# FFN tiles of 512 tokens from batch 1 on; local products one position at a time on GpSimd, sums of rows on VectorE

## The chip, the cores and the metric

The kernel runs on one core of one Trainium2 chip. The metric is the device time of one execution in microseconds; the time of a kernel is the median of its runs.

## What is computed

Eight batches of 576 tokens, eight heads of 64. Attention is the sum of a global part on rows pooled by four and a local part on the seven nearest keys; a low-rank mix over the tokens and an FFN with residual follow. All is float32.

```python
# attention, per batch and head: q, k, v are [576, 64]
q_d, k_d, v_d = (t.reshape(144, 4, 64).mean(axis=1) for t in (q, k, v))
out_up = repeat(softmax(q_d @ k_d.T / 8) @ v_d, 4)        # pooled by 4, repeated
mask = abs(pos[:, None] - pos[None, :]) < 4
out_local = softmax(where(mask, q @ k.T / 8, -1e9)) @ v
x = concat_heads(out_up + out_local)                       # [8, 576, 512]
# mix and FFN: U [576, 32], V [32, 576], w_ch1 [512, 2048], w_ch2 [2048, 512]
u = x + ((x.T @ U) @ V).T
out = u + maximum(u @ w_ch1, 0) @ w_ch2
```

## The kernel before

**FFN.** The 4608 tokens are cut into tiles, of 288 tokens in batches 0 and 1 (`NB = 2`), of 384 from batch 2 on: 4 and 9 tiles. A tile runs 16 steps, one for each 128 columns of the hidden layer. A step has `ffn1`, twelve matmuls into one bank `ps_h` (L956: four pieces `dc` of u, each as w-high x u-high, w-high x u-low, w-low x u-high), then on ScalarE the relu `hH` (L964), on VectorE the remainder `hL` (L965), and `ffn2`, twelve matmuls into the four banks `acc` (L981, three for each). `ffn2` of step i stands about `LAG` = 3 steps behind its `ffn1`. From step `H1 = NFC + LAG` on, `ps_h` alternates between two banks. `hH` has four buffers, `hL` three. At the end of a tile GpSimd adds u-high and u-low (L991), VectorE adds `acc` (L994), and the chunk `o` goes to the output. u lies in `uH` and `uL`, two buffers each.

**Attention.** Work comes in pairs of heads, four pairs a batch. The four pairs of batch 0 take an early path; the other 28 go through `late_global`, `local_attn` and `mix_part`, each pair so:
- q and k arrive as `gq` and `gT`; GpSimd adds rows by four in two steps (`pool_halves`: `gh`, then `smq` or `smk`, L440 and L442); v arrives as `vr` for each head and is added in two steps (L530, L532) into `vs`.
- TensorE makes the pooled and the local scores (L790, L783), VectorE the maximum `mx` (L540), ScalarE the exponentials `E`; TensorE transposes E (L555), multiplies by `vs` (L569); VectorE scales the result into `od` (L573); SyncE stores it to `up_s` in six DMAs (L579). The local scores go through `se` to memory and come back by position as `sc`.
- `local_attn`: nine positions per partition, `vl` holds 15 rows of v. A softmax over seven scores gives `ms`. For two positions at a time GpSimd multiplies seven rows of `vl` by `ms` into `Pt` (L852, 896 elements, the ninth position alone with 448), ScalarE copies the pooled output `ul` into the eighth place of `Pt` (L846), VectorE sums the eight places into `acc` (L857).
- `mix_part`: the sum goes to memory and comes back in two layouts; `xT` (transpose, L921), `ps_hu` (L931), then `ps_u` (the u matmul, L739), VectorE adds (L743), ScalarE writes u-high (L746), GpSimd u-low (L748).

**Order.** The program records operations with an engine, an estimated duration, a priority and the keys they read and write. A planner (`Plan.run`) simulates five engines with these numbers and issues the operations in the order it finds. Attention has lower priority numbers than the FFN matmuls, so an attention matmul goes first as soon as the plan takes it for ready, and FFN blocks fill the rest. A buffer of a pool is handed out in recorded order when its last user is done. SyncE issues every DMA. On the chip each engine works through its queue in the planned order.

**Deadlines.** The first `ffn1` of a tile reads u of all four pairs of every batch in it. Piece `dc` of u is written by pair `dc`, and the twelve matmuls take the pieces in order.

## Time and profile before

| | |
|---|---|
| time, median of 3 runs (lowest to highest) | 1010.79 us (1009.43 to 1011.28) |
| the profiled execution: its time, its span | 1003.93 us, 1002.2 us |
| TensorE: busy, share | 976.2 us, 97% |
| GpSimd | 571.7 us, 57% |
| VectorE | 438.3 us, 44% |
| ScalarE | 347.1 us, 35% |
| first matmul of the FFN, first of tile 2 | 63.15 us, 198.83 us |

Span is from the first to the last instruction of the profiled execution. Busy time of TensorE counts matmuls that overlap in its pipeline, so what a matmul costs is read from the distance of blocks in the chain, not from its own duration. "Idle before" and "waited" name what came last of the things that an instruction waited for. L956 is line 956 of the kernel before; in the changed kernel the same work has other line numbers (L949 ffn1, L974 ffn2, L958 hL, L742 the u matmul, L848 the products, L853 their reduce).

### The profile page before, as it was taken

Reading aid. Unit: us, or ns where it says so; the run is one execution under the profiler, and the core shown is the slowest. Engines: PE = TensorE matmul, PEld = TensorE weight load, DVE = VectorE, ACT = ScalarE, POOL = GpSimd, SP = SyncE. Lnnn points to the kernel's source line nnn. Section 1 sums busy time; section 2 is a strip of 40 time slices with the busy share of each in tenths; the row PEclk is TensorE's granted clock in tenths of the full one; section 3 lists DMA queues with packets and bytes.
Section 4 is the critical chain, followed back from the end, with each engine's and each line's share of the span. In section 5 each row is a group of like instructions: output and inputs, shape, how many; then the busy total and the mean of one; then the engine's idle time right before and its main releaser. Section 6 shows DMA issues by size and latency. Waiting matters only on the chain.

```text
span 1002.2 us, 24561 instructions
## 1 busy us (share of the span) xinstructions
PE 976.2 (97%) x9896; PEld 942.6 (94%) x9896; DVE 438.3 (44%) x814; ACT 347.1 (35%) x1012; POOL 571.7 (57%) x640
## 2 busy tenths in 40 slices
...
GB/s 265 317 186 210 205 154 155 154 162 137 131 121 111 130 167 130 132 105 179 144 116 128 102 137 144 83 127 113 113 150 72 32 56 24 32 2 1 32 1 32
DMA packets 220906, 120.04 MB, mean 120 GB/s; under 512 B 174052, under 2 KB 196920, under 8 KB 220792
## 3 DMA queue, kind: packets, MB, share of 16 engines
...
q14 instruction: 36, 0.29, 0.1%
...
## 4 chain that ended last, share of the span: by engine, by line
PE 86%; DMA 2%; POOL 1%; DVE 1%; ACT 1%; SPq 1%; issue 0%; DVEq 0%; ACTq 0%
PE ps_h L956 38%; PE acc L981 38%; PE ps_a L569 2%; PE ps_b L790 2%; DMA wr<-in_W 2%; PE ps_b L783 2%; PE ps_t L555 2%; PE ps_hu L931 2%; POOL Pt L852 1%; PE ps_u L739 1%; DMA vr<-in_v 1%; SPq L806 1%; DVE acc L857 0%; ACT half L347 0%; ACT E L544 0%
## 5 line engine op out<-in xcount | busy, mean ns | idle before, releaser
L981 PE MATMUL acc<-hH,W 128*128 128x384 f32 (+1 forms) x1664 | 442.3, 327 | 0.0
L956 PE MATMUL ps_h<-uH,W 128*128 128x384 f32 (+1 forms) x1376 | 360.4, 323 | 3.9 <-DVE hL L965 2.9
L981 PEld LDWEIGHTS acc<-hH,W 128*128 128x128 f32 x1664 | 297.3, 188 | 2.4
L981 PE MATMUL acc<-hL,W 128*128 128x384 f32 (+1 forms) x832 | 268.0, 322 | 0.0
L852 POOL TENSOR_TENSOR Pt<-vl,ms 128x896 f32<-128x896 f32 (+1 forms) x140 | 239.6, 1790 | 28.4 <-DMA vl<-in_vp 14.0
L956 PEld LDWEIGHTS ps_h<-uH,W 128*128 128x128 f32 x1376 | 246.3, 190 | 5.7 <-DVE hL L965 3.5
L965 DVE SCALAR_TENSOR_TENSOR hL<-ps_h,hH 128x384 fp32r<-128x384 f32 (+1 forms) x208 | 108.9, 524 | 324.1 <-ACT hH L964 323.8
L964 ACT ACTIVATE hH<-ps_h 128x384 fp32r<-128x384 f32 (+1 forms) x208 | 97.3, 468 | 366.8 <-PE ps_h L956 358.9
L956 PE MATMUL ps_h<-uL,W 128*128 128x384 f32 (+1 forms) x688 | 221.7, 322 | 1.1 <-POOL uL L748 1.1
L857 DVE TENSOR_REDUCE acc<-Pt 128x128 f32<-128x1024 f32 (+1 forms) x140 | 152.8, 1108 | 62.3 <-ACT Pt L846 27.1
L981 PEld LDWEIGHTS acc<-hL,W 128*128 128x128 f32 x832 | 156.7, 188 | 0.0
L956 PEld LDWEIGHTS ps_h<-uL,W 128*128 128x128 f32 x688 | 130.6, 190 | 1.7 <-POOL uL L748 1.7
L956 PE MATMUL ps_h<-u,W 128*128 128x384 f32 x432 | 98.1, 334 | 0.0
L923 POOL TENSOR_TENSOR xL<-xL,xH 116x640 fp32r<-116x640 f32 x28 | 43.9, 1567 | 73.4 <-ACT xH L922 66.8
L846 ACT ACTIVATE Pt<-ul 128x128 f32<-128x128 f32 (+1 forms) x140 | 56.6, 433 | 81.7 <-DVE acc L857 54.9
L991 POOL TENSOR_TENSOR o<-uH,uL 128x384 f32<-128x384 f32 (+1 forms) x43 | 39.0, 940 | 70.0 <-DMA out_t<-o 70.0
L956 PEld LDWEIGHTS ps_h<-u,W 128*128 128x128 f32 x432 | 76.9, 188 | 0.0
L748 POOL TENSOR_TENSOR uL<-xT,uH 128x384 fp32r<-128x384 f32 (+2 forms) x52 | 41.0, 808 | 56.7 <-ACT uH L746 56.7
L530 POOL TENSOR_TENSOR vr<-vr 72x256 f32<-72x256 f32 x56 | 41.2, 736 | 52.4 <-DMA vr<-in_v 51.7
L362 POOL TENSOR_TENSOR W<-c,W 128x512 fp32r<-128x512 f32 x32 | 41.0, 1289 | 14.3 <-ACT W L358 14.3
L743 DVE TENSOR_TENSOR xT<-ps_u,xT 128x384 f32<-128x384 f32 (+2 forms) x64 | 27.4, 452 | 37.2 <-PE ps_u L739 37.1
L790 PE MATMUL ps_b<-smk,smq 64*32 64x144 f32 x672 | 38.9, 296 | 0.0
...
## 6 DMA issues: line engine op xcount, KB each, us to landing
...
```

The lines of the kernel that those rows point to most:

```text
L362: pool_tt(1.0 * n, lambda: nc.gpsimd.tensor_tensor(out=lo_out(), in0=ta()[l0:], in1=hi_out()[l0:].bitcast(F32), op=ALU.subtract), [t, *own ...
L530: pool_tt(256, lambda x=x: nc.gpsimd.tensor_tensor(out=x()[:, :, 0:2, :], in0=x()[:, :, 0:2, :], in1=x()[:, :, 2:4, :], op=ALU.add), [x], ...
L748: pool_tt(n, lambda uH=uH, uL=uL, uf=uf, us=us: nc.gpsimd.tensor_tensor(out=uL.ap(hp, us), in0=uf(), in1=uH.ap(hp, us).bitcast(F32), op=AL ...
L790: nc.tensor.matmul(pg()[m:m + QL, a * SD:(a + 1) * SD], sq()[o, n:n + QL], sk()[o], start=True, stop=True)
L846: act(n * D, lambda n=n, ps=ps, Pt=Pt: nc.scalar.activation(Pt()[:, :n, :, 7], ul()[:, ps, :], AF.Copy), [ul], [(Pt, 1)], prio, 0.16)
L852: nc.gpsimd.tensor_tensor(out=Pt()[:, :n, :, 0:7].rearrange("p s d o -> p o s d"), in0=win, in1=at()[:, ps, :].rearrange("p s o -> p o s") ...
L857: dve(8.5 * n * D, lambda n=n, ps=ps, Pt=Pt: nc.vector.tensor_reduce(out=acc()[:, ps, :], in_=Pt()[:, :n], axis=AX.X, op=ALU.add), [(Pt, 0 ...
L923: pool_tt(640, lambda: nc.gpsimd.tensor_tensor(out=xL(), in0=xL().bitcast(F32), in1=xH().bitcast(F32), op=ALU.subtract), [xL, xH], [xL], prio)
L956: nc.tensor.matmul(ps()[:, :tn], W1[fc]()[:, w, dc, :], u.ap(dc), start=(n == 0), stop=(n == 3 * NDC - 1))
L964: last_h[i] = act(tn, lambda: nc.scalar.activation(hH()[:, :tn], ps()[:, :tn], AF.Relu), [ps], [hH], FIRST, 0.05)
L965: dve(tn, lambda: nc.vector.scalar_tensor_tensor(hL()[:, :tn], ps()[:, :tn], 0.0, hH()[:, :tn].bitcast(F32), op0=ALU.max, op1=ALU.subtract ...
L981: nc.tensor.matmul(ac[e]()[:, :tn], W2[fc]()[:, w, es], hx()[:, :tn], start=(fc == 0 and n == 0), stop=(fc == NFC - 1 and n == 2))
```

## The change

- **Tiles.** `NB = 1`, `TW = 512`: two tiles of 288 for batch 0, then seven of 512 and a last one of 448, ten in all. u of a tile lies in one buffer (288) or in two halves (512); the buffers of even tiles from 2 on are in pool `loc`, the others in `ffn`, two each. `LAG` is 2, `hH` and `hL` have two buffers.
- **Local part.** One position a time: GpSimd multiplies seven rows of `vl` by `ms` into `Pt` (448 elements, nine times), VectorE sums the seven places into row p of `vl` itself, and when all nine are there, one addition over 576 elements puts `ul` to them. ScalarE's copies are gone. `Pt` shares three buffers (`cT`) with the weight conversion and the output chunks; `vl` and `ul` have two buffers.
- **Sums of four rows** of late pairs: one VectorE reduce each for q, k and v of each head, in place of GpSimd's two additions.
- `od` lies in the first part of `E`; `se` is one buffer instead of two; the plan takes longer durations for three attention blocks of TensorE.

```diff
@@ attn_mix_ffn_kernel
-    TN, TW = 288, 384
-    NT = S // TN
-    NB = 2
+    TN, TW = 288, 512
+    NT = 2
+    NB = 1
...
-    LAG = 3
+    LAG = 2
...
+    def pool_late(raw, lo, out, prio):
+        dve(S, lambda: nc.vector.tensor_reduce(
+            out=out()[:, 0:SD], in_=raw()[:, lo:lo + S].rearrange("p (j r) -> p j r", r=4), axis=AX.X, op=ALU.add),
+            [raw], [out], prio)
...
-        pool_halves(qr, 0, sq, False, prio)
-        pool_halves(kr, (SPAD - S) // 2, sk, False, prio)
+        pool_late(qr, 0, sq, prio)
+        pool_late(kr, (SPAD - S) // 2, sk, prio)
...
-            pool_tt(256, lambda x=x: nc.gpsimd.tensor_tensor(
-                out=x()[:, :, 0:2, :], in0=x()[:, :, 0:2, :], in1=x()[:, :, 2:4, :], op=ALU.add), [x], [x], prio)
-            pool_tt(128, lambda x=x, vs=vs: nc.gpsimd.tensor_tensor(
-                out=vs(), in0=x()[:, :, 0, :], in1=x()[:, :, 1, :], op=ALU.add), [x], [vs], prio)
+            dve(512, lambda x=x, vs=vs: nc.vector.tensor_reduce(
+                out=vs(), in_=x().rearrange("p a r d -> p a d r"), axis=AX.X, op=ALU.add), [x], [vs], prio)
...
-        op(PE, 0.52, t_mm, [(E, a) for a in range(NQ)] + ["ident"], pt, prio)
+        op(PE, 0.6, t_mm, [(E, a) for a in range(NQ)] + ["ident"], pt, prio)
...
-        od = g([128, NQ, D], "od")
+        od = lambda: E()[:, 0:NQ * D].rearrange("p (a d) -> p a d", a=NQ)
...
-        for i in range(2):
+        for i in range(1):
             se = buf(loc, [128, NH * KL + 3], F32, f"se{i}")
...
-        for p0 in range(0, NPOS, 2):
-            n = min(2, NPOS - p0)
-            Pt = buf(loc, [128, 2, D, 8], F32, "Pt", "Pt", 2)
...
+        for p in range(NPOS):
+            Pt = buf(ffn, [128, D, 8], F32, "Pt", "cT:p", 3)
...
+                nc.gpsimd.tensor_tensor(
+                    out=Pt()[:, :, 0:7].rearrange("p d o -> p o d"), in0=vl()[:, p:p + 7, :],
+                    in1=at()[:, p, :].unsqueeze(2).broadcast_to([128, 7, D]), op=ALU.mult)
...
+            dve(7 * D, lambda p=p, Pt=Pt: nc.vector.tensor_reduce(
+                out=vl()[:, p, :], in_=Pt()[:, :, 0:7], axis=AX.X, op=ALU.add), [Pt], [(vl, p)], prio)
+        dve(1.4 * NPOS * D, lambda: nc.vector.tensor_tensor(out=ul(), in0=vl()[:, 0:NPOS, :], in1=ul(), op=ALU.add),
+            [ul] + [(vl, p) for p in range(NPOS)], [ul], prio)
...
-        hH = buf(ffn, [128, TW], F32R, "hH", bufs=4)
-        hL = buf(ffn, [128, TW], F32R, "hL", bufs=3)
+        hH = buf(ffn, [128, TW], F32R, "hH", bufs=2)
+        hL = buf(ffn, [128, TW], F32R, "hL", bufs=LAG)
```

How it moves instructions, at the start of tile 2 first. TensorE's queue before (`ps_hu` and `ps_u` are batch 1's last pair; `W_15` is the last step of tile 1, `W_0` the first of tile 2):

```order
L981 MATMUL acc_2490<-hH,W_15_2124 128x288
L931 MATMUL ps_hu<-xH,Ust 64x128 x5
L931 MATMUL ps_hu<-xL,Ust 64x128 x5
L739 MATMUL ps_u<-Vst,stk 128x288 x2
L956 MATMUL ps_h<-uH,W_0_273 128x288
L956 MATMUL ps_h<-uL,W_0_273 128x288
L956 MATMUL ps_h<-uH,W_0_273 128x288 x2
```

TensorE's queue now, from the same pair's first u matmul on:

```order
L742 MATMUL ps_u<-Vst,stk 128x512
L974 MATMUL acc_2579<-hH,W_14_2244 128x288
L974 MATMUL acc_2579<-hL,W_14_2244 128x288
L974 MATMUL acc_2579<-hH,W_14_2244 128x288
L974 MATMUL acc_2555<-hH,W_15_2305 128x288
L974 MATMUL acc_2555<-hL,W_15_2305 128x288
L974 MATMUL acc_2555<-hH,W_15_2305 128x288
L974 MATMUL acc_2562<-hH,W_15_2305 128x288
L974 MATMUL acc_2562<-hL,W_15_2305 128x288
L974 MATMUL acc_2562<-hH,W_15_2305 128x288
L742 MATMUL ps_u<-Vst,stk 128x64
```

Six more matmuls of `ffn2` follow and then tile 2's first twelve: fifteen matmuls of tile 1 now stand between the pair's first u matmul and the block that reads it.

VectorE's queue in the midst of the attention, from one `hL` to the next, before (384 columns):

```order
L965 SCALAR_TENSOR_TENSOR hL<-ps_h,hH 128x384
L857 TENSOR_REDUCE acc<-Pt 128x128
L936 TENSOR_TENSOR stk<-ps_hu,stk 32x128
L857 TENSOR_REDUCE acc<-Pt 128x128
L857 TENSOR_REDUCE acc<-Pt 128x64
L965 SCALAR_TENSOR_TENSOR hL<-ps_h,hH 128x384
```

and now, one of the fullest such stretches:

```order
L958 SCALAR_TENSOR_TENSOR hL<-ps_h,hH 128x512
L576 TENSOR_TENSOR E<-ps_a,ri 112x192
L834 TENSOR_REDUCE lsm<-ms 128x9
L535 TENSOR_REDUCE vs<-vr 72x128
L836 RECIPROCAL lrl<-lse 128x9
L853 TENSOR_REDUCE vl<-Pt 128x64
L543 TENSOR_REDUCE mx<-ps_b 128x3
L853 TENSOR_REDUCE vl<-Pt 128x64 x4
L535 TENSOR_REDUCE vs<-vr 72x128
L853 TENSOR_REDUCE vl<-Pt 128x64
L958 SCALAR_TENSOR_TENSOR hL<-ps_h,hH 128x512
```

Between two `hL` stand more and smaller operations of a pair, the sums of v among them.

GpSimd's queue, one pair's sums and products before:

```order
L440 TENSOR_TENSOR gh<-gq 128x288
L442 TENSOR_TENSOR smq<-gh 128x144
L440 TENSOR_TENSOR gh<-gT 128x288
L442 TENSOR_TENSOR smk<-gh 128x144
L530 TENSOR_TENSOR vr<-vr 72x2x128
L852 TENSOR_TENSOR Pt<-vl,ms 128x7x128 x2
L852 TENSOR_TENSOR Pt<-vl,ms 128x7x64
```

and now a pair's softmax and its nine products, with no sum near them:

```order
L829 TENSOR_TENSOR ms<-sc,lmx 128x63
L838 TENSOR_TENSOR ms<-ms,lrl 128x63
L848 TENSOR_TENSOR Pt<-vl,ms 128x7x64 x9
L829 TENSOR_TENSOR ms<-sc,lmx 128x63
L838 TENSOR_TENSOR ms<-ms,lrl 128x63
```

The sums have left GpSimd's queue, and the products come in nine pieces instead of five.

## Rows read from the trace of the kernel before

**Rows 1.** The engines' busy time, share of the span and instructions (the page's first part), and the view of cores: span and mean granted TensorE clock.

```profile
PE 976.2 (97%) x9896; PEld 942.6 (94%) x9896; DVE 438.3 (44%) x814; ACT 347.1 (35%) x1012; POOL 571.7 (57%) x640
core 0: 1002.2 us, clock 0.986
```

**Rows 2.** The chain of work that ended last (the page's fourth part): share of the span by engine, then by line.

```profile
PE 86%; DMA 2%; POOL 1%; DVE 1%; ACT 1%; SPq 1%; issue 0%; DVEq 0%; ACTq 0%
PE ps_h L956 38%; PE acc L981 38%; PE ps_a L569 2%; PE ps_b L790 2%; DMA wr<-in_W 2%; PE ps_b L783 2%; PE ps_t L555 2%; PE ps_hu L931 2%; POOL Pt L852 1%; PE ps_u L739 1%; DMA vr<-in_v 1%; SPq L806 1%; DVE acc L857 0%; ACT half L347 0%; ACT E L544 0%
```

**Rows 3.** The same chain in order of time, two neighbouring pieces in tile 9, whose tiles have 384 columns: start us, us, engine, line and matmuls in the piece.

```profile
770.08 2.08 PE ps_h L956 x12
772.16 2.08 PE acc L981 x12
```

**Rows 4.** The chain of the stretch from 200 to 300 us in order of time, two neighbouring pieces in tile 3, with 288 columns; columns as in rows 3.

```profile
287.06 1.60 PE ps_h L956 x12
288.65 1.58 PE acc L981 x12
```

**Rows 5.** The timeline of TensorE at the start of tile 2: start us, us, engine, line, operation, out<-in; in brackets the idle time before and what ended it.

```profile
198.50 0.50 PE L739 MATMUL ps_u<-Vst,stk 128*128 128x288 f32 x2 [1.55 <-DVE stk L936]
198.83 0.29 PE L956 MATMUL ps_h<-uH,W 128*128 128x288 f32 x1
...
201.22 0.40 PE L956 MATMUL ps_h<-uH,W 128*128 128x288 f32 x1 [1.03 <-ACT uH L746]
202.21 0.41 PE L956 MATMUL ps_h<-uL,W 128*128 128x288 f32 x1 [0.59 <-POOL uL L748]
```

**Rows 6.** Who TensorE waited for from 63 us to the end: engine and line that waited, what ended the wait; us in total, times, longest us. The first, the fourth and the last of eight rows, whose totals sum to 9.4 us.

```profile
PE ps_h L956 <- DVE hL L965: 2.9, 2, 2.3
...
PE ps_h L956 <- ACT uH L746: 1.0, 1, 1.0
...
PE ps_t L555 <- DVE xT L743: 0.3, 1, 0.3
```

**Rows 7.** Groups of GpSimd's instructions by line and shape: out<-in, shapes, count, busy us, mean ns of one, and idle time before them with what ended it.

```profile
L852 POOL TENSOR_TENSOR Pt<-vl,ms 128x896 f32<-128x896 f32 x112 | 212.3, 1963 | 27.3 <-DMA vl<-in_vp 14.0 <-DVE acc L857 12.7
...
L530 POOL TENSOR_TENSOR vr<-vr 72x256 f32<-72x256 f32 x56 | 41.2, 736 | 52.4 <-DMA vr<-in_v 51.7 <-PE ps_h L956 0.7
...
L852 POOL TENSOR_TENSOR Pt<-vl,ms 128x448 f32<-128x448 f32 x28 | 30.7, 1095 | 1.1 <-DVE acc L857 1.1
...
L532 POOL TENSOR_TENSOR vs<-vr 72x128 f32<-72x128 f32 x56 | 25.8, 460 | 1.6
L440 POOL TENSOR_TENSOR gh<-gq 128x288 f32<-128x288 f32 x28 | 18.9, 675 | 12.2 <-DMA gq<-in_qT 12.2
L440 POOL TENSOR_TENSOR gh<-gT 128x288 f32<-128x288 f32 x28 | 18.7, 669 | 7.0 <-DMA gT<-in_kT 5.6
...
L442 POOL TENSOR_TENSOR smk<-gh 128x144 f32<-128x144 f32 x32 | 13.7, 427 | 1.5
...
L442 POOL TENSOR_TENSOR smq<-gh 128x144 f32<-128x144 f32 x28 | 11.9, 426 | 1.6
```

**Rows 8.** Groups of VectorE's instructions by line and shape; columns as in rows 7.

```profile
L857 DVE TENSOR_REDUCE acc<-Pt 128x128 f32<-128x1024 f32 x112 | 134.8, 1216 | 60.7 <-ACT Pt L846 27.1 <-POOL Pt L852 25.1 <-issue 4.4
L965 DVE SCALAR_TENSOR_TENSOR hL<-ps_h,hH 128x384 fp32r<-128x384 f32 x144 | 79.9, 555 | 278.2 <-ACT hH L964 278.1
L965 DVE SCALAR_TENSOR_TENSOR hL<-ps_h,hH 128x288 fp32r<-128x288 f32 x64 | 29.0, 453 | 45.9 <-ACT hH L964 45.7
...
L857 DVE TENSOR_REDUCE acc<-Pt 128x64 f32<-128x512 f32 x28 | 18.9, 674 | 1.6 <-POOL Pt L852 1.5
...
L540 DVE TENSOR_REDUCE mx<-ps_b 128x3 f32<-128x432 f32 x28 | 16.9, 604 | 24.3 <-PE ps_b L783 23.9 <-PE ps_b L790 0.4
...
L573 DVE TENSOR_TENSOR od<-ps_a,ri 112x192 f32<-112x192 f32 x28 | 9.8, 351 | 12.2 <-PE ps_a L569 12.1
```

**Rows 9.** Groups of ScalarE's instructions by line and shape; columns as in rows 7.

```profile
L964 ACT ACTIVATE hH<-ps_h 128x384 fp32r<-128x384 f32 x144 | 70.9, 493 | 308.0 <-PE ps_h L956 300.4 <-PE ps_u L739 7.4
L846 ACT ACTIVATE Pt<-ul 128x128 f32<-128x128 f32 x112 | 47.2, 458 | 59.7 <-DVE acc L857 33.0 <-DMA ul<-up_s 25.6 <-POOL xL L923 0.8
...
L846 ACT ACTIVATE Pt<-ul 128x64 f32<-128x64 f32 x28 | 9.3, 333 | 22.0 <-DVE acc L857 21.9
```

**Rows 10.** VectorE's instructions of line 366, each with two SBUF inputs: count, duration ns min/median/max, first and last start us, shapes.

```profile
L366 DVE SCALAR_TENSOR_TENSOR Vst<-cv,Vst x2: 487/638/790, 22.0 to 24.9; 32x288 fp32r<-32x288 f32 x2
L366 DVE SCALAR_TENSOR_TENSOR Ust<-cu,Ust x1: 1200/1200/1200, 67.2 to 67.2; 116x160 fp32r<-116x160 f32 x1
```

**Rows 11.** Two stretches, the first from the FFN's first matmul to tile 2, the second on to the last tile that attention fills: length, then busy us and instructions of PE, PEld, DVE, ACT, POOL, then the granted clock, the DMA engines' share and GB/s.

```profile
63.00:198.80 135.80, 129.76 (x1574) 125.20 (x1574) 81.70 (x152) 67.10 (x190) 112.51 (x127) 0.96 0.74 183
198.80:865.00 666.20, 663.89 (x6517) 647.45 (x6516) 290.99 (x526) 222.00 (x670) 408.62 (x448) 1.00 0.49 115
```

**Rows 12.** Who waited for whom, all engines; columns as in rows 6.

```profile
DVE acc L857 <- POOL Pt L852: 26.6, 36, 2.6
```

**Rows 13.** The timeline of one late pair's od: VectorE's row, then SyncE's issue of the stores (columns as in rows 5).

```profile
445.67 0.35 DVE L573 TENSOR_TENSOR od<-ps_a,ri 112x192 f32<-112x192 f32 x1
446.04 3.81 SPq L579 DMA_DIRECT2D up_s<-od  x6
```

More of the change, by code (lines that the diff above doesn't have):

```diff
@@ L436, in attn_mix_ffn_kernel, with pool_halves @@
     heads = [slice(hh * D, (hh + 1) * D) for hh in range(2)]
-    def pool_halves(raw, lo, out, e, prio):
-        gh = work(e, glo, [128, SD, 2], F32, "gh")
+    def pool_late(raw, lo, out, prio):
+        dve(S, lambda: nc.vector.tensor_reduce(
+            out=out()[:, 0:SD], in_=raw()[:, lo:lo + S].rearrange("p (j r) -> p j r", r=4), axis=AX.X, op=ALU.add),
+            [raw], [out], prio)
+    def pool_halves(raw, lo, out, prio):
+        gh = work(True, early_pool, [128, SD, 2], F32, "gh")
         x4 = lambda: raw()[:, lo:lo + S].rearrange("p (j r) -> p j r", r=4)
@@ L447, in early_global @@
         sk = work(True, glo, [128, SD], F32, "smk")
[L448 to L449 removed]
+        pool_halves(qt, 0, sq, prio)
+        pool_halves(kt, (SPAD - S) // 2, sk, prio)
         od = buf(early_pool, [128, NQ, D], F32, "od_e", None, NOD)
@@ L570, in a_mm @@
                                          start=(c == 0), stop=(c == 1))
-        op(PE, 0.85, a_mm, [(E, "T", 0), (E, "T", 1)] + vss, [pa], prio)
-        od = g([128, NQ, D], "od")
+        op(PE, 1.1, a_mm, [(E, "T", 0), (E, "T", 1)] + vss, [pa], prio)
+        od = lambda: E()[:, 0:NQ * D].rearrange("p (a d) -> p a d", a=NQ)
         dve(NQ * D, lambda: nc.vector.tensor_tensor(
             out=od()[:NP], in0=out()[:NP], in1=ri()[:NP].unsqueeze(2).broadcast_to([NP, NQ, D]), op=ALU.mult),
-            [pa, ri], [od], prio)
+            [pa, ri], [(E, "od")] + [(E, "T", c) for c in range(2)] + [(E, a) for a in range(NQ)], prio)
         def store(hh):
@@ L582, in late_global @@
         for hh in range(2):
-            dma(lambda hh=hh: store(hh), [od], [(up_s, hh)], prio, 160, 1.3)
+            dma(lambda hh=hh: store(hh), [(E, "od")], [(up_s, hh)], prio, 160, 1.3)
         return s_s
@@ L859, in local_attn, with prod @@
-        dma(lambda: nc.sync.dma_start(out=x_s().rearrange("h (c s) d -> (h c) s d", s=NPOS), in_=acc()),
-            [(acc, p) for p in range(0, NPOS, 2)], [(x_s, 0), (x_s, 1)], prio)
+        for p in range(NPOS):
+            Pt = buf(ffn, [128, D, 8], F32, "Pt", "cT:p", 3)
+            def prod(p=p, Pt=Pt):
+                nc.gpsimd.tensor_tensor(
+                    out=Pt()[:, :, 0:7].rearrange("p d o -> p o d"), in0=vl()[:, p:p + 7, :],
+                    in1=at()[:, p, :].unsqueeze(2).broadcast_to([128, 7, D]), op=ALU.mult)
+            rd = [vl, at] + [(vl, i) for i in range(p, min(p + 7, NPOS))]
+            pool_tt(7 * D, prod, rd, [Pt], prio, 1.75)
+            dve(7 * D, lambda p=p, Pt=Pt: nc.vector.tensor_reduce(
+                out=vl()[:, p, :], in_=Pt()[:, :, 0:7], axis=AX.X, op=ALU.add), [Pt], [(vl, p)], prio)
@@ L862, in attn_mix_ffn_kernel @@
+        dve(1.4 * NPOS * D, lambda: nc.vector.tensor_tensor(out=ul(), in0=vl()[:, 0:NPOS, :], in1=ul(), op=ALU.add),
+            [ul] + [(vl, p) for p in range(NPOS)], [ul], prio)
+        dma(lambda: nc.sync.dma_start(out=x_s().rearrange("h (c s) d -> (h c) s d", s=NPOS), in_=ul()),
+            [ul], [(x_s, 0), (x_s, 1)], prio)
     tiles, segs = [], {}
     for g0 in (*range(0, NB * S, TN), *range(NB * S, B * S, TW)):
-        n = TN if g0 < NB * S else TW
+        n = TN if g0 < NB * S else min(TW, B * S - g0)
```

46 lines of the change are left out of this document (13 added, 33 removed).

## The prediction, made before the changed kernel was run

> **What bounds the kernel now.** I read the engines' shares first: TensorE is busy for 97% of the span at a mean granted clock of 0.986, GpSimd 57%, VectorE 44%, ScalarE 35% [rows 1]. Then the chain that ended last: 86% of it is TensorE, and the two FFN matmul lines, L956 and L981, are 38% each [rows 2]. So nearly the whole span is one queue of matmuls that waits for almost nothing: from 63 us on, when the FFN begins, its waits are eight rows that sum to 9.4 us, the largest 2.9 us, the last 0.3 us [rows 6]. The other engines count only where TensorE waits for them. The one place where it does so in a lump is the start of tile 2 at 198.5 us, where batch 1's last pair comes late: 1.55 us before its u matmul, then 1.03 and 0.59 us inside the first ffn1 [rows 5].
>
> What a matmul costs I read off the chain's blocks of twelve. At 384 columns a block takes 2.08 us [rows 3], so 173.3 ns a matmul; 384 columns at the upper clock, 2.4 GHz, are 160.0 ns, which leaves 13.3 ns. At 288 columns a block takes 1.59 us (mean of the two rows) [rows 4], so 132.5 ns, of which 120.0 are columns and 12.5 are left. The remainder hardly depends on the width: it is a price per matmul.
>
> **Fewer, wider matmuls.** Each tile has 16 steps of one ffn1 and one ffn2 block, 32 blocks of twelve. Before: four tiles of 288 and nine of 384, so 4 x 32 x 1.59 + 9 x 32 x 2.08 = 203.5 + 599.0 = 802.6 us. After: two of 288, seven of 512 and a last one of 448. With 13.3 ns a matmul a block of 512 takes 12 x (213.3 + 13.3) = 2.72 us and one of 448 2.40 us: 101.8 + 7 x 32 x 2.72 + 32 x 2.40 = 787.8 us. The term is **-14.7 us**; the columns are the same, 1152 of 4992 matmuls go. No row shows 512 columns. If the remainder grew with the width (2.08 x 512/384 = 2.77 us and 2.43 us), the stage would take 800.6 us and the gain would be 1.9 us; if it stayed at 12.5 ns, 2.71 and 2.39 us, 785.3 us and 17.3 us. I take 13.3 ns: the rows at the two widths differ by 0.8 ns only, and 384 is the nearer.
>
> The Trainium skill (TensorE: Matmul & The Clock Gate, section Back-to-back issue gap) gives N/2.4 + 2.5 ns for an isolated warm matmul. By that the 1152 matmuls would be worth 2.9 us instead of 14.7. The rows above differ from it, 13.3 and 12.5 ns, and the measurement decides; the page's form, columns plus a constant, is the one that they show.
>
> **GpSimd.** Per late pair the products are four of 896 elements at 1963 ns and one of 448 at 1095 ns, 8.95 us; afterwards nine of 448, 9.86 us. What goes are the four-row sums: two vr at 736, two vs at 460, gh at 675 and 669, smq at 426, smk at 427 ns, 4.59 us [rows 7]. Net -3.7 us a pair, about -103 us over 28 pairs: its busy time falls from 572 to about 470 us. In the stretch ahead of tile 2 it was busy for 112.5 of 135.8 us [rows 11], and the last pair of batch 1 ran through it, so this is where its relief counts: the order now has the last pair's u matmul ahead of fifteen matmuls of ffn2, not right ahead of tile 2's first block. They are 15 x 132.5 ns = 2.0 us, and the first nine of the twelve ffn1 matmuls don't read that pair, 9 x 226.6 ns = 2.0 us more of cover. The wait of tile 2's start goes: **-3.2 us** (0 if VectorE only takes GpSimd's place there).
>
> **VectorE.** It gets what the others lose. Before, a pair's reduces are four of 1216 and one of 674 ns, 5.54 us. From the two forms, (1216 - 674)/512 = 1.06 ns an element, a reduce of 448 is an estimated 606 ns and one of 576 742 ns. After: 9 x 0.61 for the products, 2 x 0.74 for q and k, 2 x 0.67 for v, and one addition of 576, from the hL rows (555 + 192 x 1.06) 0.76 us: 9.05 us [rows 8]. That is +3.5 us a pair, about +98 us; busy some 535 us. From 198.8 to 865 us it was busy for 291 of 666 us [rows 11]; 22 pairs more make it 57%. By shares there is room. But the order is dense in places: in the piece quoted in the section on the change, between two hL, stand six product reduces, two v sums, a maximum (604 ns) and od (351 ns), 5.9 us, with hL at 512 columns (an estimated 0.69 us) 6.6 us, and two small ones; the step itself is 5.44 us plus attention's matmuls.
>
> The added addition reads two SBUF tensors while GpSimd works. Of the three operations of that kind, one of 160 elements took 1200 ns though two of 288 took 487 and 790 ns [rows 10]. So it may cost up to about 1 us more a pair, on VectorE alone. The Trainium skill (SBUF — State Buffer, section Who interferes with whom) has a rule that speaks against this piece: a VectorE instruction with two SBUF inputs and a GpSimd instruction that reads SBUF lock each other out; the 1200 ns fit it. No term of the sum hangs on it.
>
> **What pays for that.** hH has two buffers instead of four: the relu of step i may start only when ffn2 of step i-2 has ended, and its bank is wanted two blocks later, after 5.44 us. ReLU (493 ns at 384 columns, so at most 0.66 us) and hL (0.69 us) leave about 4.1 us [rows 8, 9]; before it was three blocks of 2.08 less 1.05, 5.2 us. A delay of VectorE above 4.1 us stops TensorE. I charge **+2 us**: a third of the 6.2 us of waits that are left once tile 2's are gone; bounds 0 and, if these waits triple, +12.
>
> **Edits that I cost at nothing.** ScalarE's copies into Pt, 458 and 333 ns, 56.5 us in all [rows 9], go; TensorE waited for ScalarE once, 1.0 us [rows 6]. od now lies in E: it was written at 445.67 us and its six stores were issued until 449.85 us [rows 13], so the next pair's exponentials may wait some 4 us plus the landing; cover is the FFN block that TensorE always has, without it each pair would lose that. The products share three buffers with the output chunks: at eight tile ends they wait for a store. One band buffer instead of two, 16-step tiles with LAG 2 and 40 output stores for 52 change nothing on TensorE; the 64 u matmuls stay 64. The deadline of attention stays loose: batch 2's last u matmul for tile 3 stands after step 10 of tile 2, five steps or 27 us early.
>
> **Sum.** -14.7 - 3.2 + 2.0 = -15.9 us. The profiled execution took 1003.93 us, its span 1002.2 and 1.7 around it, so 988 us for one like it; the median of the runs, 1010.79, lies 6.9 us above that execution, and I carry the difference over unchanged: **995 us**.
>
> **Rivals.** *The width pays per column.* Then 1.9 + 3.2 us are won: 1005.7 us. For it: no row at 512. Against it: 12.5 and 13.3 ns. The skill's 2.5 ns would end near the same place, 1004.7 us.
> *New waits eat the gain in part or whole.* TensorE stands 8 to 11 us more than I charge, 1003 to 1006 us, or some 14 to 18, 1009 to 1013 us. For it: dense stretches of VectorE as above. Against it: before, GpSimd was as full (112.5 of 135.8 us), and TensorE hardly waited.
> *VectorE paces the FFN.* Place: hL behind the product reduces in VectorE's queue. A product takes 1095 ns and its reduce 606 ns, so a reduce that stands too early in the queue waits 0.49 us for each product, 4.4 us a pair, and hL stands behind it; before, reduces already waited 26.6 us for products, up to 2.6 us at a time [rows 12]. It decides from 4.1 us a step on; if each of the 24 pairs of batches 2 to 7 costs TensorE 1.3 us (half of that longest wait), it is 31 us, and the time 1010.8 - 17.9 + 31 = 1024 us, slower. Below 0.75 us a pair it stays faster. Against it: between the reduces stand other operations, and 57% is no bound.
>
> **How the numbers follow.** My forecast 0.70; per column 0.06; the gain eaten in part 0.05, eaten whole 0.05; slower by VectorE 0.11; 0.03 for an end below 985 us. What a measurement can tell from no change is about 0.2%, 2 us, so faster means below 1008.8 us: 0.70 + 0.06 + 0.05 + 0.03 = 0.84; same 0.05; slower 0.11. The range: the low end takes 17.3 and 3.2 us, no charge, and 5 us won of what else the first 200 us lose, 985 us; the high end takes in the per-column case and the part-eaten one, 1006 us. What lies outside is 0.11 + 0.05 + 0.03 = 0.19.
>
> **What would show it.** Right: in the chain, blocks of twelve at 2.72 us; no wait over 0.5 us at tile 2's first block; GpSimd near 470, VectorE near 535 us; TensorE's waits from 63 us on below 12 us; a span near 986 us. Wrong: blocks above 2.75 us (per column), or rows in which ps_h or a matmul of attention waits for hL, vs, smq or smk for more than 20 us together (VectorE).

## The result, and the profile after

The changed kernel took 1017.15 us (median of 4 runs, 1015.15 to 1018.32) where the kernel before took 1010.20 (4 runs, 1009.43 to 1011.28). The ratio is 1.0077, 95% interval 1.0052 to 1.0102: slower by 0.8%, where 995 us had been forecast. The profiled execution took 1018.32 us.

The engines' shares, the chain's share by engine and the clock of the changed kernel, to be read beside [rows 1, 2]:

```profile
PE 977.1 (96%) x8744; PEld 817.1 (80%) x8744; DVE 535.0 (53%) x1006; ACT 289.6 (28%) x824; POOL 459.4 (45%) x514
PE 62%; DMA 8%; DVE 6%; SPq 5%; POOL 5%; issue 3%; ACT 1%; DVEq 0%; ACTq 0%; POOLq 0%
core 0: 1016.5 us, clock 0.981
```

VectorE's 535 and GpSimd's 459 us are near the 535 and 470 us of the prediction. The chain is another: TensorE's share of it fell from 86% to 62%, and DMA, VectorE, SyncE's queue and GpSimd came in. The two stretches of [rows 11], of after (the boundary is again tile 2's start):

```profile
66.80:212.40 145.60, 136.37 (x1700) 130.25 (x1699) 113.35 (x222) 61.45 (x179) 97.86 (x107) 0.94 0.80 192
212.40:843.90 631.50, 621.71 (x5229) 503.31 (x5228) 351.28 (x648) 167.07 (x493) 306.31 (x339) 1.00 0.50 115
```

Tiles 0 and 1, which the change doesn't resize, take 145.6 us in place of 135.8, with VectorE at 113.4 of them (81.7 before) and the clock at 0.94 (0.96). By the ends of these windows, 3.8 us are lost up to the first FFN matmul, 9.8 in tiles 0 and 1, and 0.7 from there to the end: 14.3 us in all. That is more than the 7 us between the medians, since the first trace of before was 6.3 us under its median and that of after 1.2 us above. Nor are the 9.8 us all lost: the stretch now holds 126 more matmuls (1700 in place of 1574), the attention of one more pair, which later tiles don't have to make room for.

Who TensorE waits for from the FFN's start on (columns as in [rows 6]), the first seven of 13 rows, which sum to 19.5 us in place of 9.4:

```profile
PE ps_t L558 <- DVE xT L746: 3.8, 3, 1.9
PE ps_b L793 <- DVE smk L438: 2.5, 2, 1.6
PE acc L974 <- DVE hL L958: 2.0, 1, 2.0
PE ps_a L572 <- ACT E L561: 2.0, 1, 2.0
PE ps_a L572 <- DVE vs L535: 1.9, 2, 1.5
PE ps_hu L924 <- POOL xL L916: 1.6, 2, 1.1
PE ps_h L949 <- DVE hL L958: 1.4, 3, 0.5
```

14.9 us of them are waits for VectorE (5.8 before). What VectorE itself waits for, its rows with a DMA as releaser, all of the same view:

```profile
DVE vs L535 <- DMA vr<-in_v: 29.4, 18, 5.0
...
DVE lmx L828 <- DMA sc<-s_s: 15.9, 11, 3.2
DVE smq L438 <- DMA gq<-in_qT: 13.6, 9, 3.3
DVE xT L914 <- DMA Y<-x_s: 12.1, 7, 3.9
...
DVE smk L438 <- DMA gT<-in_kT: 5.0, 7, 1.1
...
DVE ul L855 <- DMA ul<-up_s: 3.4, 5, 1.0
```

79.4 us, 57 times, where the same rows of before make 15.3 us, 12 times. One place shows what that does. VectorE's timeline, then TensorE's, then three windows around it (columns as in [rows 5, 11]):

```profile
177.66 1.04 DVE L535 TENSOR_REDUCE vs<-vr 72x128 f32<-72x512 f32 x1 [3.59 <-DMA vr<-in_v]
178.62 0.20 DVE L836 RECIPROCAL lrl<-lse 128x9 f32<-128x9 f32 x1
178.74 0.39 DVE L958 SCALAR_TENSOR_TENSOR hL<-ps_h,hH 128x288 fp32r<-128x288 f32 x1
179.91 0.75 DVE L438 TENSOR_REDUCE smq<-gq 128x144 f32<-128x576 f32 x1 [0.78 <-DMA gq<-in_qT]
180.58 0.81 DVE L746 TENSOR_TENSOR xT<-ps_u,xT 128x512 f32<-128x512 f32 x2
```

```profile
179.19 0.40 PE L974 MATMUL acc<-hL,W 128*128 128x288 f32 x1 [2.04 <-DVE hL L958]
...
181.32 1.49 PE L558 MATMUL ps_t<-ident_sb,E 128*72 128x128 f32 x6 [1.60 <-DVE xT L746]
```

```profile
160.00:179.00 19.00, 17.14 (x235) 16.37 (x233) 13.18 (x30) 5.22 (x20) 10.64 (x13) 1.00 0.73 142
179.00:183.00 4.00, 2.21 (x10) 1.83 (x11) 3.22 (x7) 1.44 (x5) 3.92 (x5) 0.61 1.15 283
183.00:200.00 17.00, 17.00 (x215) 16.50 (x217) 12.39 (x27) 4.24 (x12) 12.53 (x16) 0.89 0.58 136
```

VectorE stands 3.59 us before a sum of v, because its rows haven't landed. hL is the second instruction behind it, so TensorE stands 2.04 us; then the same with q's sum and xT, 1.60 us. The granted clock falls to 0.61 in this window, a mix of its two levels of 1.2 and 2.4 GHz, and is 0.89 in the next 17 us: here the two waits cost more than their length.

VectorE's groups by shape (columns as in [rows 7]), the new ones but smk, which is as smq:

```profile
L853 DVE TENSOR_REDUCE vl<-Pt 128x64 f32<-128x448 f32 x252 | 150.0, 612 | 44.3 <-POOL Pt L848 42.8
...
L535 DVE TENSOR_REDUCE vs<-vr 72x128 f32<-72x512 f32 x56 | 60.9, 1088 | 29.5 <-DMA vr<-in_v 29.4
L855 DVE TENSOR_TENSOR ul<-vl,ul 128x576 f32<-128x576 f32 x28 | 24.4, 870 | 3.9 <-DMA ul<-up_s 3.4
...
L438 DVE TENSOR_REDUCE smq<-gq 128x144 f32<-128x576 f32 x28 | 20.7, 741 | 13.6 <-DMA gq<-in_qT 13.6
```

And the chain in order of time: two neighbouring pieces of tile 7, whose operand lies in u, two of tile 8, in uo, and one of the last tile, with 448 columns (columns as in [rows 3]):

```profile
752.95 2.72 PE ps_h L949 x12
755.67 2.72 PE acc L974 x12
...
910.33 2.79 PE ps_h L949 x12
913.12 2.73 PE acc L974 x12
...
932.44 2.43 PE ps_h L949 x12
```

### The profile page after: what moved, and what is told of

Its sections match the earlier page's. It is cut to its first block, busy times and chain, and to the rows that moved or that the text cites. A ratio compares the mean times of both kernels' runs of the same rounds, so it can differ in the third digit from the quotient of the medians.

```text
span 1016.5 us, 21910 instructions
## 1 busy us (share of the span) xinstructions
PE 977.1 (96%) x8744; PEld 817.1 (80%) x8744; DVE 535.0 (53%) x1006; ACT 289.6 (28%) x824; POOL 459.4 (45%) x514
## 4 chain that ended last, share of the span: by engine, by line
PE 62%; DMA 8%; DVE 6%; SPq 5%; POOL 5%; issue 3%; ACT 1%; DVEq 0%; ACTq 0%; POOLq 0%
PE ps_h L949 28%; PE acc L974 28%; SPq L582 3%; POOL Pt L848 3%; DMA gT<-in_kT 2%; DMA s_s<-se 2%; DVE vl L853 2%; PE ps_a L572 1%; PE ps_t L558 1%; PE ps_hu L924 1%; PE ps_b L793 1%; DVE o L987 1%; DMA vr<-in_v 1%; DMA out_t<-o 1%; PE ps_b L786 1%
## 5 line engine op out<-in xcount | busy, mean ns | idle before, releaser
L974 PE MATMUL acc<-hH,W 128*128 128x512 f32 (+2 forms) x1280 | 409.1, 377 | 0.0
L848 POOL TENSOR_TENSOR Pt<-vl,ms 128x448 f32<-128x448 f32 x252 | 244.6, 1088 | 23.6 <-DMA out_t<-o 10.7
L949 PE MATMUL ps_h<-u,W 128*128 128x512 f32 (+2 forms) x1152 | 242.1, 360 | 1.9 <-DVE hL L958 1.4
L958 DVE SCALAR_TENSOR_TENSOR hL<-ps_h,hH 128x512 fp32r<-128x512 f32 (+2 forms) x160 | 101.2, 633 | 262.8 <-ACT hH L957 260.5
L974 PE MATMUL acc<-hL,W 128*128 128x512 f32 (+2 forms) x640 | 236.8, 370 | 2.0 <-DVE hL L958 2.0
L949 PEld LDWEIGHTS ps_h<-u,W 128*128 128x128 f32 x1152 | 200.7, 192 | 29.3 <-DVE hL L958 2.1
L957 ACT ACTIVATE hH<-ps_h 128x512 fp32r<-128x512 f32 (+2 forms) x160 | 88.4, 552 | 410.6 <-PE ps_h L949 409.8
L949 PE MATMUL ps_h<-uo,W 128*128 128x512 f32 x768 | 189.8, 395 | 0.0
L853 DVE TENSOR_REDUCE vl<-Pt 128x64 f32<-128x448 f32 x252 | 150.0, 612 | 44.3 <-POOL Pt L848 42.8
L949 PEld LDWEIGHTS ps_h<-uo,W 128*128 128x128 f32 x768 | 143.4, 188 | 33.2
L535 DVE TENSOR_REDUCE vs<-vr 72x128 f32<-72x512 f32 x56 | 60.9, 1088 | 29.5 <-DMA vr<-in_v 29.4
L984 POOL TENSOR_TENSOR o<-u 128x512 f32<-128x512 f32 (+2 forms) x24 | 26.5, 1125 | 86.9 <-DMA out_t<-o 82.9
L547 ACT ACTIVATE E<-ps_b,nb 128x144 f32<-128x144 f32 x84 | 31.0, 377 | 25.5 <-DMA up_s<-E 24.1
```

The lines of the kernel that those rows point to most:

```text
L535: dve(512, lambda x=x, vs=vs: nc.vector.tensor_reduce(out=vs(), in_=x().rearrange("p a r d -> p a d r"), axis=AX.X, op=ALU.add), [x], [vs] ...
L547: act(SD, lambda a=a: nc.scalar.activation(Ea()[:, a], pooled_view(ps)[:, a], AF.Exp, bias=nb()[:, a:a + 1], scale=1.0 / 128.0, accum_out= ...
L848: nc.gpsimd.tensor_tensor(out=Pt()[:, :, 0:7].rearrange("p d o -> p o d"), in0=vl()[:, p:p + 7, :], in1=at()[:, p, :].unsqueeze(2).broadca ...
L853: dve(7 * D, lambda p=p, Pt=Pt: nc.vector.tensor_reduce(out=vl()[:, p, :], in_=Pt()[:, :, 0:7], axis=AX.X, op=ALU.add), [Pt], [(vl, p)], prio)
L949: nc.tensor.matmul(ps()[:, :tn], W1[fc]()[:, w, dc, :], u.ap(dc), start=(n == 0), stop=(n == 3 * NDC - 1))
L957: last_h[i] = act(tn, lambda: nc.scalar.activation(hH()[:, :tn], ps()[:, :tn], AF.Relu), [ps], [hH], FIRST, 0.05)
```

## The experiments

Theory 1: the sums moved to VectorE, and their waits, hold up hL and attention, and TensorE waits. Theory 2: the width's gain was lost (uo, early tiles). Other rivals: buffers coupled by the edits; the planner's order. All times are against runs of the kernel before on the same chip (medians 1009.1 to 1010.8), as a ratio with its 95% interval.

**The edits on the old tiles.** In e1 the kernel before gets all attention edits of the diff and keeps its tiles; e2, e3 and e4 get one part each; e12 is e3 with two buffers for Pt alone.

```diff
 e2: -pool_halves(qr, 0, sq, False, prio)   +pool_late(qr, 0, sq, prio)      (and kr; v as in the diff)
 e3: products and their sums as in the diff, Pt in "cT:p"
 e4: -od = g([128, NQ, D], "od")            +od = lambda: E()[:, 0:NQ * D]...  (and one se)
 e12: as e3, -Pt = buf(ffn, ..., "cT:p", 3) +Pt = buf(loc, ..., "Pt", 2)
```

> The kernel before with its tiles (288 and 384 tokens) and buffers of the FFN left as they were, and all of the change's attention edits: products one position at a time, sums of four rows on VectorE, the attention's output in E, one buffer for the banded scores. Theory 1 (the new sums and their places in VectorE's row come late, and TensorE waits for them): slower than before by 5 to 12 us, 1015 to 1022. Theory 2 (the width itself lost its gain: the pitch of matmuls on the tiles in uo, the early tiles): no slower than before, 1009 to 1012.

> The kernel before with the sums of four rows of q, k and v on VectorE as the only edit. Theory 1, with the sums as its main part: VectorE has some 85 us more and GpSimd some 100 less, TensorE's waits from 63 us on grow from 9.4 us to 14 or more, 1014 to 1018. Theory 1 with the couplings (E, cT) as its main part, and theory 2: 1008 to 1011, since VectorE stays near 45%.

> The kernel before with the products one position at a time, summed into v's rows, in the buffers that output chunks share, as the only edit. If the products' chain in v's rows or the shared buffers are what comes late (theory 1, this part): 1012 to 1016, with waits of xT, xL and scores in place of those of before. Else 1008 to 1011.

> The kernel before with the attention's output in E and one buffer for the banded scores as the only edit. If the wait of the exponentials for the stores of up_s (24.1 us in the changed kernel, up to 4.9 at a time) reaches TensorE: 1012 to 1015. If it lies beside other work, as the prediction had it: 1009 to 1011.

> The kernel before with the products one position at a time as the only edit, as in e3, but in two buffers of their own in place of the three that output chunks share. If the sharing with the output chunks (10.7 us of GpSimd's waits in the changed kernel, one of 7.7) is what cost 15 us in e3: 1009 to 1013. If it is the longer row of small instructions, each with its hand-over to VectorE: 1020 to 1026.

Measured: e1 1042.11 us, 1.0296 (1.0262 to 1.0330); e2 1018.91, 1.0087 (1.0064 to 1.0110); e3 1024.35, 1.0146 (1.0123 to 1.0170); e4 1035.97, 1.0255 (1.0231 to 1.0278); e12 1013.52, 1.0031 (1.0007 to 1.0055). Every edit costs by itself, 9, 15 and 26 us; e1, e3 and e4 lie beyond every range that either theory had for them, e2 just above its own. Together they cost 33 us and not 50, so none of these is a fixed price of its edit. With all the edits the wide tiles are some 25 us faster than the old ones (after against e1). That is more than the 14.7 us of the matmuls: TensorE's waits differ too, 29.9 us in e1 and 19.5 in after.

e2 shows most plainly what moving the sums does. Two rows of VectorE's waits in it:

```profile
DVE vs L535 <- DMA vr<-in_v: 35.0, 16, 4.1
DVE smq L438 <- DMA gq<-in_qT: 14.3, 6, 7.7
```

TensorE's waits grow by 7.7 us, those for VectorE from 4.8 to 14.8, and the time by 9.

Of the products' 15 us some 12 are the shared buffers. GpSimd's wait for output chunks in e3, which has no row in e12:

```profile
POOL Pt L845 <- DMA out_t<-o: 19.9, 6, 7.9
```

Most of e4's loss stands at one place. First TensorE's largest wait there, then SyncE's queue from 360 to 415 us, then two windows:

```profile
PE ps_a L569 <- POOL vs L532: 11.8, 3, 9.4
```

```profile
SPq L579 <- DVE E L573: 10.5, 2, 10.2
```

```profile
408.00:420.00 12.00, 2.11 (x28) 1.62 (x27) 2.97 (x5) 2.51 (x8) 7.93 (x9) 0.64 1.00 249
420.00:440.00 20.00, 12.19 (x150) 9.73 (x147) 9.85 (x17) 6.94 (x23) 14.61 (x14) 0.70 0.54 124
```

SyncE's queue stood 10.2 us before the stores of od; the load of v's rows for the next sum was queued behind them, with q's, k's and four output stores, so vs came 9.4 us late. In these 32 us TensorE was busy for 14.3, at a clock of 0.64 and 0.70. e1 has the same edit, and from the FFN on no wait of TensorE in it is longer than 3.9 us: the jam came with the order that e4's row of instructions has, and isn't a price of the edit in every order.

**Undoing single things on the wide tiles.** e5: 128 bytes free ahead of uo. e6: v's sum as two additions on VectorE. e7: v's sum back on GpSimd. e8: the planner is given the durations that the trace of after shows.

```diff
 e5: +pad = buf(loc, [128, 32], F32, "pad")
 e6: -dve(512, ... tensor_reduce(... "p a r d -> p a d r"))  +dve(256, ... tensor_tensor(...)), dve(128, ... tensor_tensor(...))
 e7: -dve(512, ...)                                          +pool_tt(256, ...), pool_tt(128, ...)
 e8: dve 512 -> 980 (v), 7 * D -> 523 (Pt), S -> 646 (q, k); products 1.75 -> 2.1 ns a column
```

> The changed kernel with 128 bytes left free ahead of the buffers in loc, so that uo begins at byte 195232 of a partition in place of 195104 (the same place within 256 bytes as the other u buffers, which begin at 144544); nothing else is edited. If the address makes the pitch of 229 to 237 ns on the uo tiles (227 on the other tiles of 512): these tiles come to 227 ns, some 3 to 5 us less than the changed kernel, 1012 to 1014. If not (traffic of other engines on the same memory, or the place in the span): the pitch stays, 1016 to 1018.

> The changed kernel with the sum of four rows of v as two additions on VectorE (256 and 128 columns, contiguous runs of 64) in place of one reduce over a strided view (1088 ns each, 56 times). Theory 1 (VectorE's late sums hold the attention and hL): VectorE some 15 to 25 us less, TensorE's waits less by 2 to 4 us, 1013 to 1015. Theory 2 (couplings, pitch and the early tiles are what costs): within 1 us of the changed kernel.

> The changed kernel with the sum of four rows of v back on GpSimd, as before the change. Theory 1: VectorE 61 us less, the waits for vs and a part of those for hL go, 1011 to 1014. If GpSimd's queue then holds the products: 1016 to 1020. Theory 2: within 1 us of the changed kernel.

> The changed kernel with only the planner's figures altered: the v sum, the products, their sums and the sums of q and k are planned at what the trace of the changed kernel measures (1088, 1088, 612 and 740 ns). If the row of instructions is out of step with the chip because these were planned too short: TensorE's waits less by 3 to 6 us, 1011 to 1014. If not: 1015 to 1019, either sign.

Measured: e5 1016.15, 1.0053 (1.0027 to 1.0080); e6 1034.22, 1.0224 (1.0182 to 1.0266); e7 1011.05, 1.0003 (0.9976 to 1.0029); e8 1015.45, 1.0051 (1.0021 to 1.0081). A block of e5's in tile 8 of the chain:

```profile
855.30 2.72 PE ps_h L951 x12
```

All uo tiles come to 2.72 us, which is worth 4 x 16 x 0.07 = 4.5 us in the trace; the times don't separate e5 from the changed kernel. The other traces agree: in the chains of after, e6, e7 and e8, which have these tiles without the 128 bytes, 42 to 50 blocks take 2.78 to 2.80 us; in those of e5, e9, e10, e14, e15 and e16, which have the bytes, at most two. e8 stays where its second reading had it, so the planned durations aren't what costs.

e7 gives back the whole loss against before, though not the forecast gain. GpSimd then waits for v's rows:

```profile
POOL vr L535 <- DMA vr<-in_v: 90.1, 22, 8.3
```

TensorE's waits fall from 19.5 to 14.8 us, those for VectorE from 14.9 to 9.5. VectorE's own waits for loads hardly fall, from 79.4 to 73.3 us, since others grow where v's are gone (15.9 and 3.4 us in after):

```profile
DVE lmx L830 <- DMA sc<-s_s: 28.4, 15, 5.4
DVE ul L857 <- DMA ul<-up_s: 15.2, 8, 3.2
```

So the sum of these waits isn't what costs. That it is the instructions behind them is the reading left; no run varies them alone.

e6 failed as an experiment on load, since two additions cost as much as the reduce, and says something else:

```profile
L535 DVE TENSOR_TENSOR vr<-vr 72x256 f32<-72x256 f32 x56 | 36.8, 657 | 53.6 <-DMA vr<-in_v 53.5
L537 DVE TENSOR_TENSOR vs<-vr 72x128 f32<-72x128 f32 x56 | 24.7, 442 | 0.6
```

VectorE's work is the same (61.5 us for 60.9), its wait for v's rows is 53.5 us in place of 29.4, and the median is up by 17 us. The time followed the waiting, not the work; but the planner has other figures here too, and so another order, which this run doesn't separate.

**Combinations.** e9: e7 and e5. e10: e9 with od in its own buffer, one ul buffer, the last addition into v's rows. e11: e10 with the sums of q and k on GpSimd. e14: e9 with LAG 3 and three hL. e15: e9 with four shared "cT" buffers. e16: e9 with NB = 2.

```diff
 e10: +od = g([128, NQ, D], "od")   -ul = lb(..., "ul", bufs=2)  +ul = lb(..., "ul")
 e11: -pool_late(qr, ...)           +pool_halves(qr, ...)
 e14: -LAG = 2    +LAG = 3
 e15: -"cT:p", 3  +"cT:p", 4        (and the other two)
 e16: -NB = 1     +NB = 2
```

> The changed kernel with two edits that each gave something alone: the sum of v's four rows back on GpSimd, and 128 bytes left free ahead of uo. If the gains add (VectorE's late v sums and the pitch on the uo tiles are separate costs): 4 to 5 us less than the v sum alone, 1005 to 1008, faster than before by 0.2 to 0.5%. If the time is set by what comes late whichever way: 1009 to 1012.

> As e9, and the attention's output in a buffer of its own in place of E, paid for by one ul buffer in place of two: the last addition writes v's rows, which are then stored to x_s. If the wait of the next pair's exponentials for the stores of up_s (24.1 us in the changed kernel) reaches TensorE on these tiles too, as it did on the old ones: 3 to 8 us less than e9. If it lies beside other work on the wide tiles: within 2 us of e9, either sign by the order that the planner makes.

> As e10, and the sums of four rows of q and k back on GpSimd too, so that of the change the wide tiles and the products one position at a time are left. Theory 1 (VectorE's late sums delay scores and hL): VectorE 39 us less, 2 to 5 us less than e10, 1000 to 1005. If GpSimd, which then has some 560 us, holds the products and uL instead: no less than e10, or 2 to 4 us more.

> As e9, with FFN2 three steps behind FFN1 and three hL buffers, as before the change, paid for by one ul buffer in place of two (the last addition writes v's rows, as in e10). If the shorter lag and fewer buffers of the hidden tile make TensorE wait for hL and in the early tiles: 3 to 6 us less than e9, and tiles 0 and 1 back to some 138 us. If not: within 3 us of e9.

> As e9, with four of the buffers that products and output chunks share in place of three, paid for in the same way. If sharing them is what costs most on the wide tiles too (on the old ones it was 11 of 15 us, e3 against e12): 4 to 8 us less than e9, 1002 to 1006. If not: within 3 us of e9.

> As e9, with four tiles of 288 tokens as before and 512 only from batch 2 on (eleven tiles in place of ten: 384 more matmuls, 5.1 us at 13.3 ns each). If wide tiles from batch 1 on are what makes the first two tiles slow (144.6 us in e9, 135.7 in the first trace of before): these lose 6 to 9 us, and the time is 1 to 4 us less than e9. If the early part is slow for other reasons: 3 to 7 us more than e9.

Measured: e9 1010.15, 1.0002 (0.9977 to 1.0026); e10 1015.06, 1.0059 (1.0035 to 1.0083); e11 1017.27, 1.0073 (1.0050 to 1.0097); e14 1010.72, 1.0003 (0.9978 to 1.0027); e15 1024.01, 1.0137 (1.0108 to 1.0165); e16 1014.46, 1.0036 (1.0009 to 1.0063). No version beat the kernel before. The lag isn't it (e14). Wide tiles from batch 1 on aren't either, by the time: e16 is 4.3 us above e9, about the 5.1 us of its extra matmuls. In its trace tiles 0 and 1 take 139.8 us, though, where e9's take 144.6, so about half of the slow start went with the wide tiles. e10 and e15 loosen a buffer, pay with the second ul buffer, and are slower than e9, which neither of their readings had; e14 pays in the same way and isn't slower, so the payment by itself doesn't explain them. Taking q's and k's sums off VectorE gave nothing: e11 is 2 us above e10, as its second reading had it.

**The order.** e13 is the kernel before for a second trace; e17 and e18 alter only what the planner believes.

```diff
 e17: -return op(POOL, 0.147 + n * ns / 1000.0   +return op(POOL, 0.150 + n * ns / 1000.0
 e18: -((n / 2 if two_x else n) + 65) / 960.0     +((n / 2 if two_x else n) + 68) / 960.0
```

> The kernel before, unedited, for a second trace: its profiled execution took 1003.93 us where its runs are near 1010. Up to the first FFN matmul the row of TensorE's instructions is the same in all kernels here, yet that stretch took 59.9 us in the trace of before and 61 to 71 in the others. If the first trace of before was a lucky one there: this stretch comes to 62 to 68 us, and what follows it stays within 3 us of the first trace. If the changed kernels themselves lengthen it: near 60 us again.

> The kernel before with one figure of the planner altered: every GpSimd instruction is planned 3 ns longer (0.150 us in place of 0.147 ahead of its columns). No instruction is added, taken away or resized; the planner's rows come out in another order from TensorE's row 148 on. If the order that the old figures gave was an unusually good one, and most of what each edit cost on the old tiles (9, 15 and 27 us) is the loss of that order: 1015 to 1030. If orders are worth about the same and the edits' own work and waits cost: 1008 to 1013.

> The kernel before with every VectorE instruction planned 3 ns longer (68 in place of 65 columns ahead of its own), nothing else altered: a second draw of an order. Same two readings as e17: 1015 to 1030 if the old order was unusually good, 1008 to 1013 if orders are worth about the same.

Measured: e13 1004.03 us, one run; its stretches, from TensorE's first instruction to the FFN, to tile 2 and to the last matmul, are 60.9, 135.2 and 798.9 us (first trace 59.9, 135.7, 799.3). The first trace is repeated, not shown to be a lucky one. e17 1010.23, 1.0000 (0.9979 to 1.0021); e18 1012.43, 1.0035 (1.0015 to 1.0055). Two other orders of the same instructions cost 0 and 3.5 us, less than each edit lost on the old tiles but e12's. They are two draws only, and e4's jam shows that an order can cost more; on the wide tiles, where single edits move the time by 5 to 17 us either way, only e8 draws an order without another edit (2 us).

**All of them in one table**: sums over the rows of the waits view from 64 us on, us (times), beside the ratio. The waits are those of one profiled execution each, the ratio is that of all runs.

| kernel | ratio | VectorE waits for DMA | TensorE waits | of these for VectorE |
|---|---|---|---|---|
| before | 1 | 15.3 (12) | 8.4 | 4.8 |
| e17 | 1.0000 | 15.8 (13) | 10.1 | 7.4 |
| e13 | one run | 13.7 (11) | 9.4 | 6.2 |
| e18 | 1.0035 | 20.2 (14) | 12.1 | 8.8 |
| e12 | 1.0031 | 43.1 (25) | 10.2 | 6.0 |
| e2 | 1.0087 | 72.4 (38) | 16.1 | 14.8 |
| e3 | 1.0146 | 58.6 (33) | 21.1 | 12.5 |
| e4 | 1.0255 | 18.4 (8) | 28.2 | 10.0 |
| e1 | 1.0296 | 80.3 (52) | 29.9 | 21.8 |
| *wide:* e9 | 1.0002 | 71.4 (45) | 13.6 | 8.0 |
| e7 | 1.0003 | 73.3 (43) | 14.8 | 9.5 |
| e14 | 1.0003 | 69.3 (45) | 20.0 | 15.3 |
| e16 | 1.0036 | 79.3 (55) | 13.3 | 7.6 |
| e5 | 1.0053 | 73.7 (51) | 16.2 | 14.1 |
| e8 | 1.0051 | 86.1 (56) | 18.2 | 14.7 |
| e10 | 1.0059 | 76.2 (45) | 19.0 | 11.2 |
| e11 | 1.0073 | 79.2 (34) | 20.2 | 9.5 |
| after | 1.0077 | 79.4 (57) | 19.5 | 14.9 |
| e15 | 1.0137 | 86.9 (49) | 24.1 | 18.6 |
| e6 | 1.0224 | 106.0 (66) | 32.8 | 28.1 |

On either set of tiles the time by and large follows TensorE's waits: on the old ones 21.5 us more of them (before to e1) go with 30 us, on the wide ones 19.2 more (e9 to e6) with 22 us. At equal waits (e3 and e11) the wide tiles are 0.7% ahead. VectorE's waits for DMA don't order the kernels: e3 has fewer than e2 and is slower, e4, whose jam is in SyncE's queue, has few, and e7 and e9 have nearly as many as after. e14 is off the line: it waits as long as after, but its FFN matmuls take 8 us less, by the count of the next section (812.9 in place of 821.0 us).

## Why the prediction was wrong

**Where the forecast went.** TensorE's time can be counted from the traces: each matmul from its start to the start of the next, with the waits apart (the view of waits has 19.5 for after's 19.0). From the FFN's first matmul to the last of all, in us:

| | before | after | change | forecast |
|---|---|---|---|---|
| FFN matmuls | 823.3 | 821.0 | -2.3 | -14.7 |
| attention's matmuls | 103.7 | 106.1 | +2.4 | 0 |
| TensorE's waits | 8.4 | 19.0 | +10.6 | -1.2 |

So the forecast of -15.9 failed in two steps of about the same size, the waits and the FFN matmuls. By the same count e2, which moves the sums alone, changes the waits (15.6) and hardly the FFN matmuls (823.0).

**Fewer, wider matmuls, -14.7 us: right in the price of a block, not in what came of it.** A block of 512 takes 2.72 us, as worked out, one of 448 2.43 us for 2.40. Per column (2.77) is out: the 2.79 on uo goes with the buffer, since u and acc have 2.72 at the same width. The uo tiles gave 4.5 us of the gain back, which no row of before could show; e5 took that back. All FFN matmuls together fell by 2.3 us in after, and by 9.4 in e9, which has the 128 bytes and v's sum on GpSimd. What took the rest, in gaps too short for the view of waits, isn't settled.

**The wait at tile 2's start, -3.2 us: gone there, not won.** Behind the wait that ends at 181.32 us TensorE shows none up to 226 us, so none at tile 2's start. Waits of 2.04 and 1.60 us stand ahead of it instead, at 179 and 181 us; whether they are the same lateness isn't shown.

**VectorE's durations: three of four right.** 612, 741 and 870 ns against 606, 742 and 760 with up to 1 us more (the addition's median is 759, its longest 1694). The sum of v was priced like a contiguous reduce, 674 ns, and takes 1088 (1031 to 1118 each time): 23 us more. The Trainium skill (SBUF — State Buffer, section Door 1: The DMA port swizzle) says that each access which crosses to a new 16-byte line pays a penalty, so that four float32 are as far as one gets without it. The traces agree in direction: 741 ns for 576 elements in runs of four, 1088 for 512 that lie 256 bytes apart.

**The step that failed on the side of the waits is the charge of +2 us for VectorE**, "by shares there is room". It was a third of the 6.2 us of waits that were left, argued from busy times and the length of dense pieces. Those waits came to 19.5 us, so the charge measured 13.3 us, just past its upper bound of 12, and clock was lost behind them. What it left out stands in [rows 7]: before, GpSimd was idle 51.7 us for v's rows, 12.2 for q's and 5.6 for k's. I moved the sums and counted their work, and not these waits, which moved with them: in after VectorE waits 29.4, 13.6 and 5.0 us for the same loads. On VectorE hL, xT and the output stand in the same queue. On GpSimd little of this reached TensorE; its waits for GpSimd in the trace of before were these two rows (columns as in [rows 6]):

```profile
PE ps_h L956 <- POOL uL L748: 1.1, 2, 0.6
PE ps_a L569 <- POOL vs L532: 0.9, 2, 0.5
```

The last addition likewise took over the wait for ul that ScalarE's copies had, 25.6 us in [rows 9] and 3.4 in after.

The rival "VectorE paces the FFN" had hL behind VectorE's queue right, but put the wait at the products. Those waits grew too, from 26.6 us ([rows 12]) to 42.8, but in e7 they are 88.4 us and its time is that of before. Nor did its sign come: TensorE waited 7.8 us for hL, vs and smk, not 20. The nearest rival is "new waits eat the gain in whole", 1009 to 1013 us, and even that fell short.

That moving the sums costs is shown, by e2 for all of them on the old tiles and by e7 for v's on the wide ones. That it is their waits and not their work rests on the rows of e2 and on e6, and is in part argued. For q and k on the wide tiles e11 gave nothing back, so theirs isn't shown there. And e7 accounts for 6 of the 22 us between the forecast and the measured time; the other 16 were not won back by any run.

**Edits costed at nothing: wrong on the old tiles.** od in E and one se cost 26 us there (e4, most of it in the one jam of SyncE's in-order queue, which e1 doesn't have), shared buffers some 12 of the products' 15 (e3, e12). On the wide tiles SyncE's queue waits too:

```profile
SPq L582 <- DVE E L576: 56.7, 14, 8.2
```

But giving od its own buffer didn't help there (e10), and a fourth shared buffer hurt (e15), each paid for with a ul buffer, so on the wide tiles the cost of these edits isn't settled.

**Left open.** Both traced executions of before took 1004 us where its runs have medians near 1010. Up to the first FFN matmul TensorE's row is the same in all kernels, yet takes 60 and 61 us in these two traces and 61 to 68 in the others (64.9 in e17, whose time is that of before). From the FFN on e17 takes 934.9 us and the first trace of before 935.3, so these two differ ahead of the FFN alone; what sets that stretch isn't shown. Why loosening buffers made e10 and e15 slower is told by the table only as later operands.
